# Storing the last output tile of a fused attention and soft-MoE kernel in nine parts instead of one

## The chip, the core and the metric

The kernel runs on one NeuronCore of a Trainium2 chip. The metric is the device time of one execution in microseconds (us); the median over several executions counts. Instructions run on five engines: PE (matrix multiply), DVE (vector), ACT (scalar and activation), POOL (GpSimd) and SP, which here does nothing but issue DMAs and wait on semaphores. Data moves between HBM and the on-chip memory SBUF by DMA, on 16 DMA engines.

## What is computed

The reference is softcapped attention over 8 batches, 12 heads, 448 positions and head size 64, followed by a soft mixture of experts on the 3,584 tokens of width 768:

```python
scores = scale * np.matmul(q, k.transpose(0, 1, 3, 2))
scores = cap * np.tanh(scores / cap)
attn = softmax(scores); x = attn @ v            # as (3584, 768)
logits = x @ phi                                # 32 slots
slot_input = softmax over tokens(logits).T @ x  # 8 experts, 4 slots each
slot_out[e] = relu(slot_input[e] @ w1[e]) @ w2[e]
c = logits - logits.max(1, keepdims=True)
c = np.exp(c)
c /= c.sum(1, keepdims=True) + 1e-09
return (c @ slot_out).astype(np.float32)
```

Only the last line, the product of the 3,584 x 32 combine weights with the slot outputs, and the storing of its result touch the change.

## The kernel before

Attention fills most of the span (ACT, DVE and PE are all near 90% busy until about 230 us). Then come the slot sums, the two expert layers, and the output stage, which this document is about.

**The output stage.** The tokens are taken as 28 tiles of 128, numbered n = 0 to 27, where `bb, c = divmod(n, NT)` with NT = 7: tile n holds, for a pair of batches bb, every seventh token starting at c, so partition p of the tile is token 7p + c of the pair (896 tokens). For tiles 0 to 11 the two halves of the 768 columns are made and stored apart, by `half_tile` (L1067). For tiles 12 to 27 the loop at L1107 does the whole width: two matmuls into PSUM (L1120), then one scaling by `winv` that writes the tile `ob` in SBUF, on DVE for odd n (L1127) and on ACT for even n (L1129). Two tiles in a row share an `ob` where they can and are stored together, with 6,144 contiguous bytes per partition; a tile whose c is 6 closes its pair of batches, and may then be stored alone, with 3,072 bytes per partition. So tiles 12 to 27 give nine stores: (12, 13), (14, 15), (16, 17), (18, 19), 20, (21, 22), (23, 24), (25, 26), 27.

**The store.** `store` (L1058) issues one DMA on SP for the rows of all 128 partitions (L1061). Its `sp.dma_start` is at the same line for all 28 stores of the kernel, 19 of them from `half_tile` and nine from the loop at L1107. The engines' queues work strictly in the order of the program text; the stores are issued in the order of n.

**What orders the DMAs.** The framework gives each DMA that SP issues a completion semaphore out of eight, in rotation (in the trace's semaphore numbers 103, 104, 105, 106, 107, 109, 110, 100 and again). Before each issue SP executes an EVENT_SEMAPHORE on the semaphore that the DMA is about to use. A DMA counts as landed when its semaphore has got 16 increments. The loads of expert weights `w2t` (L994) are issued on SP just ahead of the stores, in the same rotation. At the end of the program (L1164, the closing of the tile framework) SP waits for all eight semaphores, and the engines then meet at a barrier.

Of the kernel before, what the change touches and what calls it, by code (L numbers as in the profile page):

```python
# [18 lines left out]
P = 128  # L19
HP = 64  # L20
NT = 7
DH = 64
S = 448
# [14 lines left out]
def kernel(  # L38
# [13 lines left out]
    D = H * DH  # L52
# [4 lines left out]
    HD = D // 2  # L57
# [12 lines left out]
    pe, dve, act, pool, sp = nc.tensor, nc.vector, nc.scalar, nc.gpsimd, nc.sync  # L70
# [984 lines left out]
    so_ps += [bank([P, HD], name=f"so_ps{half}") for half in range(2)]  # L1055
    obs, waiting = {}, {}

    def store(n, h0, h1, src, tokens=1):  # L1058
        bb, c = divmod(n, NT)
        width = (h1 - h0) * HD  # L1060
        sp.dma_start(out=bass.AP(tensor=out.tensor,  # L1061
                                 offset=(2 * bb * S + c) * D + h0 * HD,
                                 ap=[[NT * D, P], [1, tokens * D]] if width == D else
                                 [[NT * D, P], [D, tokens], [1, width]]),
                     in_=src)

    def half_tile(n, half, home, eng):  # L1067

        bb, c = divmod(n, NT)
        if c == 0:  # L1070
            obs[bb, half] = wts.tile([P, NT, HD], F32, name="obh", tag="w1", bufs=E)
        ob = obs[bb, half][:, c, :]
        pe.matmul(home, et_tile(bb, c), so[half], start=True, stop=True)
        if eng == "dve":
            dve.tensor_scalar_mul(ob, home, winv[:, bb, c:c + 1])
        else:
            act.mul(ob, home, winv[:, bb, c:c + 1])
        k = waiting.pop(half, n)
        if half and n + 1 < NH and c < NT - 1 and k == n:
            waiting[half] = n  # L1080
            return
        store(k, half, half + 1, obs[bb, half][:, c - (n - k):c + 1, :], n - k + 1)
# [24 lines left out]
    for n in range(B // 2 * NT):  # L1107
        bb, c = divmod(n, NT)
        if n == NH + 3:
            e_transp(B - 1)  # L1110
        if n == NH + 5:
            e_transp(B - 2)
        if n == NH + 7:
            e_sums(B // 2 - 1)
        op = fin.tile([P, 2, 512], F32, name="op", tag="op")
        if n < NH:
            half_tile(n, 1, op[:, 0, 0:HD], "act" if n % 2 else "dve")
            continue
        for half in range(2):
            pe.matmul(op[:, half, 0:HD], et_tile(bb, c), so[half],  # L1120
                      start=True, stop=True)

        if n == NH or c == 0 or full:
            ob, n1 = wts.tile([P, 2, 2, HD], F32, name="ob", tag="w1", bufs=E), n
        dst = ob[:, n - n1, :, :]
        if n % 2:
            dve.tensor_scalar_mul(dst, op[:, :, 0:HD], winv[:, bb, c:c + 1])  # L1127
        else:
            act.mul(dst, op[:, :, 0:HD], winv[:, bb, c:c + 1])  # L1129
        full = n > n1 or c == NT - 1  # L1130
        if full:
            store(n1, 0, 2, ob[:, 0:n - n1 + 1, :, :].rearrange("p t a d -> p (t a d)"),
                  n - n1 + 1)
# [35 lines left out]
```

## Time and profile before

| | |
|---|---|
| time, median of 3 runs | 287.55 us (287.51, 287.55, 289.25) |
| the profiled execution's own time | 287.83 us |
| its span (first to last instruction) | 286.1 us |
| last compute instruction ends (DVE, tile 27) | 275.8 us |
| issue of the last store on SP | 276.1 to 277.3 us |
| last store landed | 285.04 us |
| mean granted TensorE clock | 0.983 |

The span is read from the first instruction to the last; the time has 1.7 us more around it. In the span's last 10 us no compute engine has work: what is left is DMA. Times "at 276.1" are in us from the span's start, as in all views of the trace. Besides the views, the trace holds a record of each issue on SP (start, duration, semaphore), of each semaphore increment, and of each DMA packet (start, duration, size); where a number below is said to come from a record, it is one of these.

### The profile page before, as it was taken

What the parts mean: (1) busy time and instruction counts of PE and PEld (TensorE: products, weight loads), DVE (VectorE), ACT (ScalarE), POOL (GpSimd) and SP (SyncE); (2) the same over time, 40 slices, a digit from 0 to 9 for tenths busy, and PEclk for the clock granted to TensorE, in tenths of its full rate; (3) what the DMA queues carried; (4) which work ended last, traced back from release to release, by engine and by line L of the source; (5) the groups of instructions that cost most, each with busy time, mean ns of one, the idle gap of its engine ahead of it and who ended that gap; (6) DMA issues with size and microseconds to landing.
All of it is one profiled execution on the core that took longest, in us unless ns stands there. A gap on an engine that the chain in (4) does not pass through costs nothing.

```text
span 286.1 us, 10835 instructions
## 1 busy us (share of the span) xinstructions
PE 250.7 (88%) x4744; PEld 170.5 (60%) x4744; DVE 242.2 (85%) x500; ACT 254.5 (89%) x211; POOL 139.4 (49%) x197
## 2 busy tenths in 40 slices
PE   8898889998998899989998999899899999998710
PEld 7565466756675666566656675667575767642300
DVE  3498999999999999999999999999999986337740
ACT  3999999999999999999999999999999997237720
POOL 7794554764665566555655556574553120200000
PEclk9999999999999999999999999999999999999985
DMA  7999999999999999999999999999999567989995
GB/s 220 264 195 201 224 202 225 221 202 215 225 231 181 206 232 224 221 205 231 222 217 209 229 224 213 212 228 224 207 184 229 125 248 233 400 324 391 413 424 243
DMA packets 58334, 68.11 MB, mean 238 GB/s; under 512 B 4144, under 2 KB 54448, under 8 KB 58288
## 3 DMA queue, kind: packets, MB, share of 16 engines
q0 software_dynamic: 42448, 35.31, 78.8%
q1 hardware_dynamic: 15552, 31.89, 31.8%
q8 instruction: 37, 0.61, 0.8%
q10 hardware_dynamic: 288, 0.23, 0.3%
q14 instruction: 9, 0.07, 0.1%
HBM read 91.72 MB, written 19.27 MB: 388 GB/s over the span
## 4 chain that ended last, share of the span: by engine, by line
DVE 34%; PE 25%; ACT 25%; issue 7%; POOL 4%; DMA 2%; DVEq 0%; ACTq 0%
ACT ex L329 13%; ACT ex L334 10%; PE pv L590 7%; DVE xq L600 5%; PE sc L320 3%; DVE ex L571 3%; DVE xp L570 3%; DVE xp L568 3%; DVE xT L652 3%; DVE ex L564 2%; DVE qT L279 2%; DMA out_dram<-ob 2%; PE so_ps L1043 2%; DVE xp L567 2%; PE hp L1015 2%
## 5 line engine op out<-in xcount | busy, mean ns | idle before, releaser
L329 ACT ACTIVATE ex<-sc 128x1344 f16<-128x1344 f32 (+1 forms) x113 | 152.2, 1499 | 1.2 <-PE sc L320 1.2
L334 ACT ACTIVATE ex<-ex 128x2688 bf16<-128x2688 f16 (+5 forms) x58 | 119.3, 2070 | 0.1
L590 PE MATMUL pv<-vbd,ex 128*128 128x130 bf16 (+1 forms) x1610 | 95.0, 211 | 11.2 <-POOL vbd L287 8.2
L590 PEld LDWEIGHTS <-ex 128*128 128x128 bf16 (+1 forms) x1680 | 75.7, 101 | 35.9 <-PE sc L320 9.0
L320 PE MATMUL sc<-qT,kT 64*64 64x448 bf16 x672 | 71.2, 359 | 0.6 <-DVE qT L279 0.4
L287 POOL CAST vbd<-vraw 64x896 bf16<-64x896 f32 x46 | 45.8, 997 | 48.5 <-PE pv L590 21.2
L600 DVE TENSOR_TENSOR xq<-pv,rec 128x448 bf16<-128x448 f32 x46 | 28.7, 624 | 1.6
L320 PEld LDWEIGHTS <-kT 64*64 64x64 bf16 x672 | 24.1, 105 | 6.1 <-issue 4.3
L568 DVE TENSOR_TENSOR xp<-xp,xf 128x1344 f16<-128x1344 f16 (+2 forms) x34 | 25.3, 744 | 0.6
L295 POOL MEMSET vbd<- 64x1 bf16 x22 | 3.7, 166 | 45.1 <-PE pv L590 45.1
L571 DVE TENSOR_TENSOR ex<-ex,xp 128x1344 uint16<-128x1344 uint16 (+2 forms) x34 | 25.2, 742 | 0.4
L116 POOL DMA_DIRECT2D w1b<-in_moe_w_dram x32 | 25.4, 796 | 0.0
L570 DVE TENSOR_TENSOR xp<-xp,xf 128x1344 f16<-128x1344 f16 (+2 forms) x34 | 24.5, 720 | 0.8
L567 DVE TENSOR_SCALAR xp<-xf 128x1344 f16<-128x1344 uint16 (+2 forms) x34 | 17.1, 502 | 0.4
L184 POOL DMA_DIRECT2D qb<-in_q_dram x22 | 16.6, 757 | 0.8 <-DMA kraw<-in_k_dram 0.8
L279 DVE COPY kT<-kps 128x896 bf16<-128x896 bf16 x23 | 14.2, 616 | 3.0 <-PE kps L274 2.8
L572 DVE TENSOR_SCALAR ex<-ex 128x1344 uint16<-128x1344 uint16 (+2 forms) x34 | 16.5, 487 | 0.1
L620 PE MATMUL pv<-ones 128*128 128x57 bf16 x390 | 16.4, 188 | 0.0
L277 PEld LDWEIGHTS <-qb 128*64 128x64 bf16 x308 | 10.1, 109 | 10.6 <-issue 10.5
L184 POOL DMA_DIRECT2D kb<-in_k_dram x22 | 16.2, 736 | 0.0
L120 POOL DMA_DIRECT2D w2d<-in_moe_w_dram x21 | 16.0, 780 | 0.4 <-issue 0.4
L564 DVE TENSOR_SCALAR ex<-ex 128x1344 uint16<-128x1344 f16 (+2 forms) x34 | 15.7, 461 | 0.1
(121 smaller groups left out, 342.2 us busy)
## 6 DMA issues: line engine op xcount, KB each, us to landing
w1b<-in_moe_w_dram POOLq DMA_DIRECT2D x32, 384.0 KB, 8.5
vraw<-in_v_dram SPq DMA_DIRECT2D x44, 224.0 KB, 6.0
w2d<-in_moe_w_dram POOLq DMA_DIRECT2D x21, 384.0 KB, 8.5
w2t<-w2d SPq DMA_DIRECT2D x21, 384.0 KB, 6.9
out_dram<-ob SPq DMA_DIRECT2D x7, 768.0 KB, 7.8
qb<-in_q_dram POOLq DMA_DIRECT2D x22, 224.0 KB, 7.5
kb<-in_k_dram POOLq DMA_DIRECT2D x22, 224.0 KB, 6.0
w2b<-in_moe_w_dram POOLq DMA_DIRECT2D x11, 384.0 KB, 7.8
```

The costliest lines, as they stand in the source:

```text
L116: pool.dma_start(out=w1b[e][:, js, fs], in_=w1r[:, e, js, fs])
L184: pool.dma_start(out=t, in_=quad_ap(nm, Q))
L287: pool.tensor_copy(vbds[Q % 2][r, :, :, c0:c0 + DH], raw[r])
L320: pe.matmul(sc[cs, u, 0:S], qkT["k", Q][r, c, cs], qkT["q", Q][r, :, cs], start=True, stop=True)
L329: act.activation(exs[j][:, half * CS + u0:half * CS + u1, :].bitcast(F16), (own[0] if i == u0 == 0 else sc)[:, u0:u1, 0:S], ACT.Tanh, scal ...
L334: act.activation(exs[j][:, u0:u1, :], exs[j][:, u0:u1, :].bitcast(F16), ACT.Exp, scale=cap)
L567: lambda: dve.tensor_scalar(p, f, c3, c2, ALU.mult, ALU.add),
L568: lambda: dve.tensor_tensor(p, p, f, op=ALU.mult),
L570: lambda: dve.tensor_tensor(p, p, f, op=ALU.mult),
L571: lambda: dve.tensor_tensor(y, y, p, op=ALU.add),
L590: pe.matmul(out_, exs[j][r, u, q0:q0 + (HP if tail else P)], v_, start=(c == 0 and g == gs[0] < NF), stop=(c == NT - 1), skip_group_check= ...
L600: dve.tensor_tensor(xq[Q][:, h, s0:s1, :], pv[:, 0:s1 - s0, 0:DH], rec.to_broadcast([P, s1 - s0, DH]), op=ALU.mult)
```

## The change

The store of tile 27 is issued as nine DMAs of 64, 14, 12, 10, 8, 6, 4, 2 and 8 rows (128 in all), one after the other on SP. All other stores stay one DMA each. A part takes partitions r0 to r0 + rows of `ob` and writes the same bytes to the same places as before.

```diff
+    PARTS = {27: (64, 14, 12, 10, 8, 6, 4, 2, 8)}
+
     def store(n, h0, h1, src, tokens=1):
         bb, c = divmod(n, NT)
         width = (h1 - h0) * HD
-        sp.dma_start(out=bass.AP(tensor=out.tensor,
-                                 offset=(2 * bb * S + c) * D + h0 * HD,
-                                 ap=[[NT * D, P], [1, tokens * D]] if width == D else
-                                 [[NT * D, P], [D, tokens], [1, width]]),
-                     in_=src)
+        r0 = 0
+        for rows in PARTS.get(n, (P,)):
+            sp.dma_start(out=bass.AP(tensor=out.tensor,
+                                     offset=(2 * bb * S + r0 * NT + c) * D + h0 * HD,
+                                     ap=[[NT * D, rows], [1, tokens * D]] if width == D else
+                                     [[NT * D, rows], [D, tokens], [1, width]]),
+                         in_=src[r0:r0 + rows])
+            r0 += rows
```

## The prediction

> **What bounds the kernel now.** Only the end matters, since every instruction ahead of tile 27's store is the same. I read the page's 40 slices first, then the stretch table of the last 11 us, then the store's own line, then SP's waits.
>
> The stretch table says what is left when compute has ended (columns: stretch, its length, busy time of each engine, granted clock, share of the 16 DMA engines, GB/s):
>
> ```profile
> 276.00:279.00 3.00, 0.00 (x0) 0.00 (x0) 0.00 (x0) 0.00 (x0) 0.00 (x0) 0.52 1.03 426
> 279.00:282.00 3.00, 0.00 (x0) 0.00 (x0) 0.00 (x0) 0.00 (x0) 0.00 (x0) 0.50 1.02 426
> 282.00:283.00 1.00, 0.00 (x0) 0.00 (x0) 0.00 (x0) 0.00 (x0) 0.00 (x0) 0.50 0.96 387
> 283.00:285.10 2.10, 0.00 (x0) 0.00 (x0) 0.00 (x0) 0.00 (x0) 0.00 (x0) 0.50 0.07 29
> ```
>
> All engines are idle, the DMA engines are full until 283.0, and then they run at 0.07 for two more microseconds, about one engine of 16. The packet records tell more: fourteen engines send their last 4-byte semaphore packet between 282.96 and 283.13, one at 283.59 and one at 284.69. The two late ones have lagged by 0.6 and 1.6 us since the stores issued near 264.6; on all engines a row of 3,072 bytes takes 0.118 us. The last of the 16 increments comes at 285.04, 0.35 after its packet, and the program ends at 286.05, so 1.02 us of closing barrier follow.
>
> The line of the stores, the whole-width ones alone, then the first of all stores, which met a nearly empty queue, then the last one:
>
> ```profile
> L1061 SPq EVENT_SEMAPHORE  x9: 17/28/90, 266.0 to 276.1; - x9
> L1061 SPq DMA_DIRECT2D out_dram<-ob x9: 622/1163/1666, 266.1 to 276.1; - x9
> DMA to landing us min/median/max: 6.1/7.8/9.1
> ...
> L1061 SPq DMA_DIRECT2D out_dram<-obh x1: 337/337/337, 255.3 to 255.3; - x1
> DMA to landing us min/median/max: 1.9/1.9/1.9
> ...
> L1061 SPq DMA_DIRECT2D out_dram<-ob x1: 1213/1213/1213, 276.1 to 276.1; - x1
> DMA to landing us min/median/max: 8.9/8.9/8.9
> ```
>
> An issue takes SP 0.34 us when little is queued and 1.2 us behind a backlog. A store lands 1.9 us after its issue begins when little is queued, and 8.9 us at the end, because 7 us of earlier stores stand ahead of it.
>
> SP's waits in the loads just ahead of the stores (239 to 250 us), and in the closing:
>
> ```profile
> SPq L994 <- DMA w2t<-w2d: 3.7, 6, 1.0
> ...
> SPq L1061 <- DMA w2t<-w2d: 0.5, 1, 0.5
> ...
> SPq L1164 <- DMA out_dram<-ob: 7.4, 6, 1.8
> ```
>
> The first two lines carry the prediction: SP waited seven times for an earlier DMA that has nothing to do with the data of the next. In the records each such wait ends at the landing of the DMA issued eight before, on the same semaphore: landed 243.227, wait over 243.244, issue 243.291; landed 244.208, issue 244.225; landed 249.392, wait over 249.409. So at most eight DMAs of SP are in flight. In the stage of whole-width stores this never bites: 17 to 90 ns a wait, since each landed long before its semaphore came round.
>
> **The change part by part.** It removes one issue (1.21 us of SP at 276.12) and adds nine, p1 to p9, with eight more semaphore waits. Nothing else stands behind them on SP but the closing. The semaphores in turn, and the landing each part must wait for: p1 107 (272.12, over), p2 109 (273.95, over), p3 110 (275.77, over), p4 100 (277.61), p5 103 (278.56), p6 104 (280.41), p7 105 (282.28), p8 106, the store of tiles 25 and 26 (284.09), and p9 107 again, which is p1 itself.
>
> *Issues p1 to p7.* Each costs between 0.32 us (the shortest w2t issue) and 1.21 (the last store), plus 0.06 between two. By 1.27 each until the 6,144-byte packets are gone at 282.0, five are through at 282.4; for the next two I take 0.60 each, the vraw loads' figure, which also move 64 rows; p7 ends near 283.7. With 0.32 each, p7 only waits for 282.28 and ends at 282.7. Either way it is before 284.09, so I cost them at nothing; the cover is p8's wait. If all seven cost 1.27, p7 ends at 285.0 and the cover is gone (a rival below).
>
> *The rows themselves.* p1's 64 rows should be 4 on each engine instead of 8, as 128 rows are 8. The latest engine finishes them 4 x 0.118 = 0.47 us after the store of tiles 25 and 26: landed at 284.09 + 0.47 = 284.56 (the whole tile 27 took 0.95). The 64 rows of p2 to p9 are placed on engines in a way that no row of this trace shows; spread out, one row an engine, they cost the busiest engine 8 rows, 0.94 us, against the 4 it lost: fourteen engines would still end by 283.6 and the latest by 285.2 at worst, ahead of what follows. I cost them at nothing here, and bound the other case below.
>
> [...] The loads of 64 partitions (vraw) show packets of 1,792 bytes at a median of 87 ns, the first loads of 128 partitions 74 ns: 18% more, so p1 might take 0.56 instead of 0.47. [...]
>
> *p8.* It waits for 284.09, issues at 284.09 + 0.06 = 284.15 and holds SP for 0.34 (little queued) to 0.60, until 284.49 to 284.75.
>
> *p9.* It waits for p1, landed at 284.56, and issues at 284.63; with a p8 issue of 0.60 at 284.81. From issue to landing: the first store needed 1.87 with eight rows of 65 ns; with a single row of 118 ns this is 1.87 - 0.52 + 0.12 = 1.47. Low end 1.2, if a quarter of the rows also shortens the issue of 0.34 by most of itself; high end 2.15, if the issue is as long as vraw's (0.28 more than 1.87). I take 1.67, midway between 1.47 and 1.87. Landing at 284.63 + 1.67 = 286.30; ends 285.83 and 286.96.
>
> *The closing.* 1.02 us as before; the other seven semaphores are passed while SP waits for p9.
>
> The sum: 286.30 - 285.04 = +1.26 us on the profiled execution: span 287.3, own time 287.83 + 1.26 = 289.1. That execution stands 0.28 above the median, so I put the difference on the median: 287.55 + 1.25 = 288.8 us. With the ends of p9, 288.35 to 289.5. The late engine hardly matters: without its lag both p8's wait and the old end come 1.6 us sooner.
>
> **Rivals.** *The waits do not bind and the late engines gain.* If parts 8 and 9 are in the queue before 284.09 (other semaphores, or an order that passes old landings), the end is the latest engine's. With 4 rows instead of 8 it ends at 285.04 - 0.47 = 284.57: 287.1 us. For it: two engines are late and get less if the small parts miss them. Against it: seven waits at L994 and L1061 show the rotation at work. Partly hidden waits lie between it and my sum. Chance 0.12.
>
> *The issues become the bound.* Nine at 1.27: p9 begins at 276.12 + 8 x 1.27 = 286.28, its issue ends at 287.49, and 1.33 later (1.67 less the 0.34) it lands at 288.82: +3.8, 291.3 us. For it: all nine whole-width issues but one took over 1.07. Against it: at 255.3 an issue took 0.34, and the backlog is gone at 283.0. It makes the kernel slower by over 1% (+2.88) if the mean issue is 1.11 or more. Chance 0.06.
>
> *The small parts bunch on one engine.* No SP transfer here has fewer than 64 rows, so parts not a multiple of 16 might go through one engine. Then it carries 4 + 64 rows: from 282.02, where a punctual engine is done with tiles 25 and 26, 68 x 0.118 = 8.0 us, landing at 290.4: +5.4, 292.9 us. It passes 1% once about 43 of the 64 rows share one engine; less bunching gives +1.3 to +2.8. Chance 0.06. [...]
>
> **How the numbers follow.** My forecast has 0.76, of which 0.05 is for p1 at half rate (289.3 us). The range takes its own 288.35 to 289.5, down to 287.5 for waits partly hidden and run-to-run spread, up to 289.9 for mild bunching. About 1% (2.9 us) is what a measurement of this kernel can tell from no change. Faster by that much: 0.01, as even the gaining rival brings 0.16%. Slower by that much: 0.08, most of the last two rivals. Within: 0.91, my forecast (+0.4%) among it.
>
> **What would show it.** Right: nine issues at the store's line; the last two starting at about 284.15 and 284.6 after waits on a DMA; the last landing near 286.3; about 1.2 us with hardly a packet before it. Wrong: the nine issues back to back and ended before 284 (waits not binding), issues of 1.1 us and more to the end, or one engine busy with rows after 285.

## The result, and the profile after

The changed kernel takes 289.38 us (median of 14 runs, 288.72 to 290.23) against 287.65 us for the kernel before in the same comparison (14 runs, 287.10 to 289.28). The ratio is 1.0046, 95% interval 1.0031 to 1.0062: slower by 1.3 us (0.9 to 1.8), less than 1%. The two medians lie further apart, by 1.7 us; where this text turns a ratio into microseconds, it goes by the ratio. The profiled execution took 289.13 us with a span of 287.4.

The stretch table of the end, after (columns as before):

```profile
276.00:279.00 3.00, 0.00 (x0) 0.00 (x0) 0.00 (x0) 0.00 (x0) 0.00 (x0) 0.50 1.03 428
279.00:282.00 3.00, 0.00 (x0) 0.00 (x0) 0.00 (x0) 0.00 (x0) 0.00 (x0) 0.50 1.02 426
282.00:283.00 1.00, 0.00 (x0) 0.00 (x0) 0.00 (x0) 0.00 (x0) 0.00 (x0) 0.50 0.92 332
283.00:285.10 2.10, 0.00 (x0) 0.00 (x0) 0.00 (x0) 0.00 (x0) 0.00 (x0) 0.50 0.19 67
285.10:287.00 1.90, 0.00 (x0) 0.00 (x0) 0.00 (x0) 0.00 (x0) 0.00 (x0) 0.50 0.09 17
```

In the first two rows the DMA share is that of before (1.03 and 1.02). The backlog drains a little more unevenly around 283, and then a stretch is added, from 285.1 to 287, in which the DMA engines are 9% busy. Almost nothing is moved there; somebody waits. SP's issues and waits show who (the store's line is now L1065, the closing L1169). The fence has first the issues until 284, then those after it, then SP's waits from 282 on.

```profile
L1065 SPq DMA_DIRECT2D out_dram<-ob x7: 293/1149/1564, 276.3 to 283.0; - x7
...
L1065 SPq DMA_DIRECT2D out_dram<-ob x2: 236/256/277, 284.2 to 284.7; - x2
...
SPq L1065 <- DMA out_dram<-ob: 1.1, 2, 0.9
SPq L1169 <- DMA out_dram<-ob: 0.9, 2, 0.7
```

Seven parts are issued without a gap by 283.3. Then SP waits twice at the store's line for a store that is still on its way, 1.1 us in all, and issues parts p8 and p9 at 284.25 and 284.71. The records give the chain link by link:

| link | forecast, us | measured, us |
|---|---|---|
| store of tiles 25 and 26 landed | 284.09 | 284.232 |
| p8 issued, and how long SP took | 284.15, 0.34 | 284.248, 0.236 |
| p1 landed | 284.56 | 284.692 |
| p9 issued | 284.63 | 284.708 |
| p9 landed, and time from its issue | 286.30, 1.67 | 286.314, 1.606 |
| closing, last landing to the end of the span | 1.02 | 1.048 |

The last landing moved from 285.037 to 286.314, by 1.28 us. Of this 0.14 was there already when tiles 25 and 26 landed (284.089 before): they were issued 0.14 later too, at 275.09 against 274.95, by the identical program ahead of the change. So in what follows I compare from that landing on. From it to the last landing the kernel before needs 0.948 us and the changed one 2.082, a loss of 1.13.

### The profile page after: what moved, and what is told of

It reads as the page before. It is cut to its first block, busy times and chain, and to the rows that moved or that the text cites. A ratio compares the mean times of both kernels' runs of the same rounds, so it can differ in the third digit from the quotient of the medians.

```text
span 287.4 us, 10843 instructions
## 1 busy us (share of the span) xinstructions
PE 250.6 (87%) x4744; PEld 170.3 (59%) x4744; DVE 242.3 (84%) x500; ACT 254.5 (89%) x211; POOL 138.9 (48%) x197
## 4 chain that ended last, share of the span: by engine, by line
DVE 29%; PE 27%; ACT 26%; issue 9%; POOL 3%; DMA 2%; DVEq 0%; ACTq 0%
ACT ex L329 14%; ACT ex L334 11%; PE pv L590 7%; DVE xq L600 5%; PE sc L320 4%; DVE xp L570 3%; DVE ex L571 3%; DVE xT L652 3%; DVE xp L568 2%; DMA out_dram<-ob 2%; PE so_ps L1043 2%; PE hp L1015 2%; DVE ex L564 2%; DVE qT L279 2%; POOL vbd L287 2%
## 5 line engine op out<-in xcount | busy, mean ns | idle before, releaser
L329 ACT ACTIVATE ex<-sc 128x1344 f16<-128x1344 f32 (+1 forms) x113 | 147.9, 1422 | 1.2 <-PE sc L320 1.2
L334 ACT ACTIVATE ex<-ex 128x2688 bf16<-128x2688 f16 (+5 forms) x58 | 114.8, 1988 | 0.1
L571 DVE TENSOR_TENSOR ex<-ex,xp 128x1344 uint16<-128x1344 uint16 (+2 forms) x34 | 24.6, 722 | 0.4
L569 DVE TENSOR_SCALAR xp<-xp 128x1344 f16<-128x1344 f16 (+2 forms) x34 | 15.4, 454 | 0.6
```

Of the source, the lines that this page charges most:

```text
L329: act.activation(exs[j][:, half * CS + u0:half * CS + u1, :].bitcast(F16), (own[0] if i == u0 == 0 else sc)[:, u0:u1, 0:S], ACT.Tanh, scal ...
L334: act.activation(exs[j][:, u0:u1, :], exs[j][:, u0:u1, :].bitcast(F16), ACT.Exp, scale=cap)
L571: lambda: dve.tensor_tensor(y, y, p, op=ALU.add),
```

## The experiments

Theory A is that of the prediction: eight completion semaphores in rotation, so the eighth and ninth part wait for landings, and the last round trip stands in an otherwise empty DMA queue. Rival B is the time of SP's issues, rival C a cost of small transfers in themselves. All differ from the changed kernel only where the diff says, and each ratio is against runs of the kernel before on the same chip. In the table at the end of this section are the ratios and the two stretches of each trace.

**Seven parts instead of nine.**

```diff
-    PARTS = {27: (64, 14, 12, 10, 8, 6, 4, 2, 8)}
+    PARTS = {27: (64, 14, 12, 10, 8, 6, 14)}
```

> Tile 27 in seven parts of 64, 14, 12, 10, 8, 6 and 14 rows. Theory A (the rotation of eight semaphores): the seventh part's semaphore is that of tiles 23 and 24, landed at about 282.4, so no part waits for a store that is still on its way at the end, all seven are issued by 283.3, and the end is the latest DMA engine's, with 4 rows instead of 8: last landing near 284.6 to 284.7 against 285.04 before, time 0.4 us under the kernel before (ratio 0.9986). Rival B (SP's issue time, more with each part): two issues fewer than nine save about 0.6 us of the 1.3, so 0.7 us over the kernel before (1.0024). Rival C (small transfers on few engines are slow in themselves): the same 64 rows go in small parts, so 1.2 us over the kernel before (1.004).

Measured: ratio 1.0030 (1.0011 to 1.0049). Theory A's time (0.9986) is missed, and that of rival B (1.0024) is nearer; so it has to be seen in the trace which of the two is at work. There the last landing is at 284.89, 0.80 after tiles 25 and 26: 0.15 sooner than in the kernel before, not 0.4. SP's waits from 276 on hold no line of the store any more:

```profile
SPq L1169 <- DMA out_dram<-ob: 1.3, 2, 1.1
SPq L1169 <- PEq L1169: 0.7, 2, 0.5
```

The seventh issue ends at 283.07, 1.0 us before tiles 25 and 26 have landed (284.09), so SP's issues are not on the path to the last landing; B would have them there. The wait is gone, as A says, but the time is not under that of the kernel before. The span shows where 0.5 us went: from the last landing to the end it takes 1.56 us instead of 1.02. The last part's semaphore (105) stands in the middle of SP's closing waits, so the waits on 106, 107, 109 and 110 come after it, and between the last two of them the record has a gap of 0.36 us in which SP waits for nothing that the trace shows.

**Eight parts.**

```diff
-    PARTS = {27: (64, 14, 12, 10, 8, 6, 4, 2, 8)}
+    PARTS = {27: (64, 14, 12, 10, 8, 6, 4, 10)}
```

> Tile 27 in eight parts of 64, 14, 12, 10, 8, 6, 4 and 10 rows. Theory A: the eighth part waits for the landing of tiles 25 and 26 (284.1 to 284.25), is issued then and lands 1.6 us later, near 285.85: 0.75 us over the kernel before (1.0026), and over 1 us above seven parts. Rival B: one issue fewer than nine, 1.0 us over (1.0035), and 0.3 us above seven parts. Rival C: 1.2 us over (1.004), the same as seven parts.

Measured: 1.0036 (1.0015 to 1.0056). SP's waits now have the store's line again, once:

```profile
SPq L1065 <- DMA out_dram<-ob: 1.2, 1, 1.2
SPq L1169 <- DMA out_dram<-ob: 0.9, 1, 0.9
```

Tiles 25 and 26 landed at 284.868, the eighth part was issued at 284.884 and landed at 286.464, 1.58 after its issue. From tiles 25 and 26 to the last landing it is 1.60 us, against 0.80 with seven parts and 0.95 before. One part more, 64 rows in small parts in both: the step in the tail is the wait. The times alone (1.0030 and 1.0036) would not have told the two apart; the traces do.

**The last two parts on POOL's queue.**

```diff
-            sp.dma_start(out=bass.AP(tensor=out.tensor,
+            (pool if n == 27 and r0 >= 118 else sp).dma_start(out=bass.AP(tensor=out.tensor,
```

> The same nine parts, but the last two (2 and 8 rows) are issued by POOL, whose DMAs take their semaphores from another rotation. Theory A: nothing waits for a store on its way, the two are queued when tile 27 is ready, and the time is 0 to 0.4 us under the kernel before (0.9986 to 1.000). Rival B: seven issues on SP, 0.7 us over (1.0024). Rival C: the same small parts, 1.2 us over (1.004).

Measured: 1.0029 (1.0006 to 1.0053). POOL issued the two parts at 276.1 and 276.6, and they landed at 282.1 and 282.7, ahead of every other part of the tile. SP's waits from 276 on again hold no line of the store:

```profile
SPq L1169 <- DMA out_dram<-ob: 1.2, 1, 1.2
SPq L1169 <- PEq L1169: 0.7, 2, 0.5
```

The last landing is at 284.61, 0.50 after tiles 25 and 26: the same nine parts, in the same sizes, end 1.58 us sooner than on SP alone. This takes rival C out as the cause of the 1.1 us. The time, however, is again not below that of the kernel before, which A had forecast (B's 1.0024 is again nearer); the closing took 1.64 us, with a gap of 0.34 us at the same place as with seven parts (SP issues seven in both). With seven and with eight parts on SP, fifteen recorded instructions of SP lie between the wait for p1's semaphore and the gap. Counted the same way with nine parts, the place is the closing's wait for p9, where such a gap would be hidden.

**Nine parts of 16 and 8 rows.**

```diff
-    PARTS = {27: (64, 14, 12, 10, 8, 6, 4, 2, 8)}
+    PARTS = {27: (16, 16, 16, 16, 16, 16, 16, 8, 8)}
```

> Nine parts of 16, 16, 16, 16, 16, 16, 16, 8 and 8 rows, so that seven of them load all 16 engines alike. Theory A: the eighth part still waits for tiles 25 and 26, the ninth follows it 0.3 to 0.4 us later: last landing near 286.15, 1.1 us over the kernel before (1.004). Rival B: nine issues, 1.3 us over (1.0046). Rival C: with most rows spread evenly the cost goes: 0 to 0.3 us over (1.000 to 1.001).

Measured: 1.0041 (1.0023 to 1.0059). Tiles 25 and 26 landed at 285.036, the eighth part was issued at 285.053, the ninth at 285.428, and it landed 1.61 later: 2.00 us after tiles 25 and 26, as with the uneven parts (2.08). Only the eighth part waited here: the first had landed at 285.252, while the eighth was being issued (until 285.384). Between these two lists the spread of the rows makes no difference that shows; the reversed order below shows that it can.

**Two parts.**

```diff
-    PARTS = {27: (64, 14, 12, 10, 8, 6, 4, 2, 8)}
+    PARTS = {27: (64, 64)}
```

> Tile 27 in two parts of 64 rows. Theory A (the rotation of eight semaphores, now with a closing that may cost SP 0.1 more): no part waits, every DMA engine carries 4 + 4 rows, the second issue is hidden by the backlog: 0 to 0.2 us over the kernel before (1.000 to 1.0007). Rival B (issue time): 0.15 us over. Rival C, here as half rate for 64 rows: 0.5 to 0.9 us over (1.0017 to 1.003).

Measured: 1.0007 (0.9988 to 1.0026), and in the trace 0.958 us from tiles 25 and 26 to the last landing, against 0.948. Splitting as such costs nothing that shows.

**The changed kernel once more**, on the chip of the runs before and after it here.

> The changed kernel once more, so that it stands on the same chip as the other three. Theory A: 1.15 to 1.3 us over the kernel before (1.004 to 1.0045); in the trace the last two parts start 0.01 to 0.02 us after a landing, as before.

Measured: 1.0052 (1.0033 to 1.0070). Landings at 285.569 and 286.042, the last two issues at 285.586 and 286.058, landing 1.606 after: the same chain, in an execution that ran 1.3 us later as a whole.

**The parts in another order, the 64 rows last.**

```diff
-    PARTS = {27: (64, 14, 12, 10, 8, 6, 4, 2, 8)}
+    PARTS = {27: (8, 2, 4, 6, 8, 10, 12, 14, 64)}
```

> The nine parts in another order: 8, 2, 4, 6, 8, 10, 12, 14 and at the end 64 rows. Theory A: the last part is issued after the same wait, about 284.6, and has 4 rows on each engine instead of one row on eight: it lands 0.3 to 0.4 us later than the 8 rows did, so 1.5 us over the kernel before (1.005). Rivals B and C: the same parts and issues, 1.2 us over (1.004).

Measured: 1.0086 (1.0070 to 1.0102), so 2.5 us over the kernel before, not 1.5. The wait is where A puts it (tiles 25 and 26 landed at 284.611, the eighth part issued at 284.627), but the last part lands 2.62 us after its issue. Its issue took 0.55 us, and most of its rows took 0.233 us each. In the full queue of the kernel before every row of 3,072 bytes took 0.121. My account of the last transfer lacked something.

**Tile 20 in nine parts, tile 27 in one.**

```diff
-    PARTS = {27: (64, 14, 12, 10, 8, 6, 4, 2, 8)}
+    PARTS = {20: (64, 14, 12, 10, 8, 6, 4, 2, 8)}
```

> Tile 20 in the nine parts, tile 27 in one. Theory A: the eighth part waits for tiles 18 and 19 (landed at 277.6), the ninth for the first part (278.1); tiles 21 and 22 are then issued at 278.5 instead of 272.3, with the DMA queues run dry since about 276.5; three and a half stores of 0.94 and 1.87 us follow from 279.35 on, last landing near 286.25: 1.2 us over the kernel before (1.004; 0.9 to 1.6 us), with a hole of 2 to 3 us in the DMA's busy share. Rival B (each issue takes 1.2 us wherever it stands): the later stores come 10 us later, over 3 us over (1.01). Rival C: the small transfers lie beside a backlog, 0 to 0.5 us over.

Measured: 1.0053 (1.0033 to 1.0074), 1.5 us. The same wait, put into the middle of the stage, opens a hole in a full DMA queue. The stretch table of this kernel:

```profile
274.00:276.00 2.00, 1.08 (x4) 0.21 (x2) 1.20 (x2) 0.90 (x1) 0.00 (x0) 0.50 1.00 415
276.00:277.00 1.00, 0.00 (x0) 0.00 (x0) 0.74 (x1) 0.00 (x0) 0.00 (x0) 0.50 0.86 298
277.00:278.00 1.00, 0.00 (x0) 0.00 (x0) 0.00 (x0) 0.00 (x0) 0.00 (x0) 0.50 0.31 108
278.00:279.00 1.00, 0.00 (x0) 0.00 (x0) 0.00 (x0) 0.00 (x0) 0.00 (x0) 0.50 0.06 18
279.00:280.00 1.00, 0.00 (x0) 0.00 (x0) 0.00 (x0) 0.00 (x0) 0.00 (x0) 0.50 0.38 123
280.00:282.00 2.00, 0.00 (x0) 0.00 (x0) 0.00 (x0) 0.00 (x0) 0.00 (x0) 0.50 1.02 424
```

The DMA share falls from 1.00 to 0.06 and comes back at 280. In the kernel before the same microseconds are full:

```profile
277.00:278.00 1.00, 0.00 (x0) 0.00 (x0) 0.00 (x0) 0.00 (x0) 0.00 (x0) 0.50 1.00 421
278.00:279.00 1.00, 0.00 (x0) 0.00 (x0) 0.00 (x0) 0.00 (x0) 0.00 (x0) 0.50 0.98 409
279.00:280.00 1.00, 0.00 (x0) 0.00 (x0) 0.00 (x0) 0.00 (x0) 0.00 (x0) 0.50 1.02 430
```

Tiles 18 and 19 landed at 278.106, the eighth part was issued at 278.123; the first part landed at 278.575, the ninth was issued at 278.592, and the stores of tiles 21 to 26 stood behind it on SP. The last landing, 286.85, is 0.6 later than expected, of which 0.5 was there when tile 20's first part was issued (271.50 against 271.01); the time lies in A's range of 0.9 to 1.6 us. Rival B, by which every issue takes 1.2 us, is out: it asked for over 3 us, and the issues of 8 to 2 rows took 0.24 to 0.29 us once the backlog was going down.

**Where 64 rows lie.** The reversed order left open why the last 64 rows were slow. By one answer, theory A's here, it is where they lie: they were partitions 64 to 127, all in one half of the 128. Then 64 rows from both halves should take 0.121 us each again, and land 4 x (0.233 - 0.121) = 0.45 us sooner after their issue, an estimate from the two row times and four rows on each of the 16 engines. Rival D is any other reason, such as the long issue (0.55 us), by which the place makes no difference. Two kernels with the same nine sizes, eight of 8 rows and one of 64, differ only in which partitions each part has (each kernel has one of the two `PARTS` lines); for the first of them A and D ask for the same time, 2.3 us over the kernel before, for the second A asks for 1.85:

```diff
-    PARTS = {27: (64, 14, 12, 10, 8, 6, 4, 2, 8)}
+    PARTS = {27: ((0, 8), (8, 8), (16, 8), (24, 8), (32, 8), (40, 8), (48, 8), (56, 8), (64, 64))}   # e9
+    PARTS = {27: ((0, 8), (8, 8), (16, 8), (24, 8), (96, 8), (104, 8), (112, 8), (120, 8), (32, 64))}   # e10
...
-        r0 = 0
-        for rows in PARTS.get(n, (P,)):
+        for r0, rows in PARTS.get(n, ((0, P),)):
...
-            r0 += rows
```

> Nine parts: eight of 8 rows (partitions 0 to 63), then one of the 64 rows 64 to 127. [...] Time 2.3 us over the kernel before (1.008) by both.

> The same nine sizes, but the eight small parts are partitions 0 to 31 and 96 to 127, and the last one is the 64 rows 32 to 95, which lie in both halves. [...] Rival D: 2.6 us, no difference to the run before.

Measured: 1.0083 (1.0060 to 1.0106) and 1.0076 (1.0051 to 1.0100). The times don't tell the two apart, the traces do: the last part landed 2.69 us after its issue with partitions 64 to 127 and 2.24 with 32 to 95. The stretch in which only this part's rows move, first for `e9`, then for `e10`:

```profile
285.58:286.73 1.15, 0.00 (x0) 0.00 (x0) 0.00 (x0) 0.00 (x0) 0.00 (x0) 0.50 0.79 178
...
286.19:286.89 0.70, 0.00 (x0) 0.00 (x0) 0.00 (x0) 0.00 (x0) 0.00 (x0) 0.50 0.70 281
```

The same bytes take 1.15 us in one and 0.70 in the other (the fronts and ends of the stretch are partly empty in both, and in `e9` one packet of 8,192 bytes of another queue lies in it). By the packet records most rows took 0.22 to 0.24 us in `e9`, and all of them 0.119 to 0.121 in `e10`. So in these two runs the time of a row went with where the 64 rows lay, about 0.23 us in one half and 0.12 in both; by what mechanism, they do not show. Rival D's long issue is out: it was the longer one in `e10`, 0.62 us against 0.56.

**Two tries at a faster kernel.** Since part of the end is one late DMA engine (in the kernel before its last packet came 1.10 us behind the last of the other fifteen), fewer rows for it might help. I supposed that with 108 and 20 rows four DMA engines get no row of tile 27, and that with 120 and 8 rows one engine gets none; no run shows this.

```diff
-    PARTS = {27: (64, 14, 12, 10, 8, 6, 4, 2, 8)}
+    PARTS = {27: (108, 20)}   # e11
+    PARTS = {27: (120, 8)}    # e12
```

> A try at a faster kernel: two parts of 108 and 20 rows. [...] Theory A: where the latest engine is among these four, the end is no longer its 8 rows behind tiles 25 and 26: last landing 0.7 to 0.9 us sooner, 0.5 to 0.8 us under the kernel before (0.997 to 0.998); where it is not, 0.3 us over (1.001). Rival C (fewer rows a part cost in themselves): over the kernel before.

> [...] Theory A: 0.5 to 0.8 us under the kernel before if that engine is the latest in this program (0.997 to 0.998), else 0 to 0.1 us over (1.000).

Measured: 1.0017 (0.9998 to 1.0035) and 1.0012 (0.9995 to 1.0030): neither is faster. With 108 and 20 rows the trace does have the shorter end that A forecast, 0.356 us from tiles 25 and 26 to the last landing against 0.948. But tiles 25 and 26 themselves landed 0.6 us later than in the kernel before (284.715). They were issued 0.6 later already (275.53 against 274.95), ahead of the change. The median of all runs lies above that of the kernel before by 0.5 us all the same, at the edge of the interval. Whether that is chance, or whether the late engine changes from execution to execution, the single profile of each kernel does not say; it stays open. With 120 and 8 rows the same stretch took 1.14 us, longer than before.

All runs side by side. "Tail" is from the landing of tiles 25 and 26 to the last landing, "closing" from there to the end of the span, both from the one profiled execution:

| kernel | ratio to before (95% interval) | tail, us | closing, us |
|---|---|---|---|
| before | 1 | 0.95 | 1.02 |
| changed, nine parts | 1.0046 (1.0031 to 1.0062) | 2.08 | 1.05 |
| nine parts, again | 1.0052 (1.0033 to 1.0070) | 2.10 | 1.05 |
| nine parts of 16 and 8 | 1.0041 (1.0023 to 1.0059) | 2.00 | 1.05 |
| eight parts | 1.0036 (1.0015 to 1.0056) | 1.60 | 1.42 |
| seven parts | 1.0030 (1.0011 to 1.0049) | 0.80 | 1.56 |
| nine, two of them on POOL | 1.0029 (1.0006 to 1.0053) | 0.50 | 1.64 |
| two parts of 64 | 1.0007 (0.9988 to 1.0026) | 0.96 | 0.97 |
| 108 and 20 | 1.0017 (0.9998 to 1.0035) | 0.36 | 0.96 |
| 120 and 8 | 1.0012 (0.9995 to 1.0030) | 1.14 | 0.96 |
| 64 last, reversed order | 1.0086 (1.0070 to 1.0102) | 3.00 | 1.05 |
| 64 last, partitions 64 to 127 | 1.0083 (1.0060 to 1.0106) | 3.02 | 1.06 |
| 64 last, partitions 32 to 95 | 1.0076 (1.0051 to 1.0100) | 2.58 | 1.05 |
| tile 20 in nine | 1.0053 (1.0033 to 1.0074) | | 1.06 |

No version beats the kernel before. Tail and closing together are 1.16 us longer than before with nine parts, 0.39 with seven and 0.18 with two on POOL; the ratios are worth 1.3, 0.9 and 0.8 us. The last two sums lie at the lower ends of their intervals (0.3 to 1.4 and 0.2 to 1.5 us), and one execution of each doesn't show where the rest of the time goes, or whether it is there.

## Why the prediction was right, step by step

- **The waits of p8 and p9** are the cause, and their size was right: forecast +1.26 us on the last landing, measured +1.28 with 0.14 of drift, ratio worth 1.3 us. That the landing agrees to 0.02 is luck: without the drift it is 1.13. The median, 289.38, is 0.6 above the forecast of 288.8 and near the 289.3 of the half-rate case, but not for that reason (see the rows of p1 below). Eight parts instead of seven brings the wait back, POOL's queue takes it away with all parts in place, and tile 20 shows the same wait with a price worked out for another place. The forecasts of the times without the wait, at or below the kernel before, were missed. The 1% that I took for what a measurement can tell was too coarse: the intervals here reach 0.15 to 0.25% to each side.
- **Issues p1 to p7 at nothing**: right. They ended at 283.3, in the cover of p8's wait (284.25). The single issues did not go as I had put them: five took 0.81 to 1.56 us while the backlog stood, the last two 0.29.
- **Rows of p1 at 0.47**: measured 0.46. On the latest engine, which ends p1, its four rows took 0.121 us each at 283.88 to 284.36, when hardly another row moved, so the 18% of the vraw loads (0.56) did not show there. No run shows p1 at half rate, the term behind the 289.3 us and its chance of 0.05: in its place stand the 0.46 us here, and two parts of 64 rows that cost nothing that shows (0.958 us against 0.948). Rows of mostly 0.22 to 0.24 us showed where 64 rows of one half were alone in the queue (the reversed order and `e9`).
- **p9's round trip, 1.67**: measured 1.606, by two errors that cancel. I took 0.12 us for its rows; four of them took 0.364 to 0.394, and from the first row's start to the last semaphore packet it was 0.49. Against that, the first row started 0.77 us after the issue, less than the 0.84 of the first store, whose issue took 0.34 and not 0.28.
- **The closing at 1.02**: right for nine parts (1.05), but not a constant: with seven parts it was 1.56, and the 0.54 more is over three times the 0.15 that the last landing had gained on the kernel before. I had kept it at 1.02, and with p9's wait in it that holds.
- **Rivals.** The gain by lighter late engines (287.1 us): without the waits the landing did come sooner, by 0.15 us with seven parts and by 0.45 with two on POOL, and the closing took it all. Issues as the bound: out, since p7's issue ended 0.95 us before p8's began. Bunching on one engine: out. It asked for a landing at 290.4, and p2 to p7 had all landed by 284.75. In the records a part of 14 rows has 15 semaphore increments, one of 12 has 13, and so on down to 3 for 2 rows, where a store of 128 or 64 rows has 16: one a row and one more, which I read as one row an engine. The first increment of the 14-row part comes at 279.09, 0.12 us after the end of its issue, and the other 14 from 283.16 to 284.00.

## What to carry to other kernels

Count the DMAs in flight, not only their bytes: where the framework hands out completion semaphores in rotation, as here eight, DMA number i waits for the landing of number i less the rotation's length, and behind the backlog here a landing came 6.1 to 9.1 us after the issue. Look for it where a wait on a semaphore ends just behind a landing (0.017 us here) that the waiting transfer's data has nothing to do with. A split that passes the rotation paid a whole round trip here, 1.6 us, on the path to the end. Staying within it does not make a split free: two parts cost nothing that shows, but seven, without any wait for an earlier store, were still 0.9 us (0.3 to 1.4) slower, of which a longer closing explains part. Look at the closing too, and don't take the time for the mechanism: the ratios of seven and nine parts overlap, and only their traces tell them apart.

## What the runs showed of the hardware that I had not expected

- A store into an otherwise empty queue took, from issue to landing, 1.27 us for 2 rows, 1.61 for 8, 2.24 for 64 rows in both halves of the partitions and 2.62 to 2.69 for 64 rows in one half. Eight neighbouring rows took up to 0.39 us each, against 0.121 in a store of 128.
- SP's issue took 0.24 to 0.32 us for 2 to 14 rows in an idle queue, 0.55 to 0.62 for 64 rows, and 0.81 to 1.56 us for 8 to 14 rows behind a backlog. There even 2 rows took 0.99 (reversed order).
- The late DMA engine was not the same one in the profiles of different programs. In the changed kernel the part of 14 rows landed at 284.00 and p1 at 284.69, so the latest engine is none of the fourteen; its second execution agrees (285.33 and 286.04). With seven parts the part of 14 rows landed at 284.74, 0.16 after p1, and that of 12 rows at 284.04, so there it is one of the fourteen and none of the twelve. In the reversed order the part of 4 rows landed at 283.84 and that of 6 rows at 285.02, after tiles 25 and 26: there it is one of the six.
- SP stalled 0.34 to 0.36 us in the closing of the kernels with seven and eight SP parts, one wait earlier with eight than with seven. A cause that moves with the number of SP's instructions would fit; that was not tried.
